# One row of padding and one weight slice: where a matmul's two operands lie in SBUF

## The chip, the cores and the metric

The kernel runs on one core of one Trainium2 chip. The metric is device time in microseconds (us) of one execution. The core's engines are named as the profile names them: PE (TensorE matmul), PEld (TensorE weight load), DVE (VectorE), ACT (ScalarE), POOL (GpSimd), SP (SyncE, which issues the DMAs here). SBUF is the on-chip memory that all of them read; every tile has a byte address there that is the same in each of the 128 partitions.

## The reference

A causal 7-tap filter over 4096 positions (its taps are a softmax, one set for each of 8 channel groups), and then two expert layers, one with h·cos(h), one with h·relu6(h+3)/6:

```python
x = attn_out.reshape(B * S, D)          # 4 * 4096 tokens, D = 192
h = x @ w_in                            # 192 -> 2048
g = h * np.cos(h)                       # second layer: h * clip(h + 3, 0, 6) / 6
return g @ w_out                        # 2048 -> 192
```

## The kernel before

Tokens are the moving (streamed) side: 32 blocks of N = 512 tokens, two layers, and 16 steps of 128 of the 2048 hidden channels for each block and layer, 1024 steps in all. Each float32 operand is held as a high and a low float32r part, so that one product takes several passes.

A step's **first product** (`mm1`, L636) makes `h`. It is done for two steps at once: 9 passes, each a pair of matmuls. One matmul of a pair works on rows 0 to 63 of the array, the other on rows 64 to 127 (`HALF`), and the two halves run beside each other. Its moving tiles are `own`, `swap` and `last` (4096 bytes a partition, four buffers each).

The **second product** (`mm2`) takes `gh` and `gl`, the high and the low part of the activation (2048 bytes a partition, four buffers each), and adds into four PSUM accumulators: a0 and a1 (`A`) for 128 output channels, b0 and b1 (`B`) for the other 64. A step has five passes, again pairs over the two halves of the rows: A with `gh` and the high weights, A with `gh` and the low weights, B with `gh` and 128 columns (64 high, 64 low: rows 0 to 63 and 64 to 127 of b hold the two, and are added at the end), A with `gl`, and B with `gl`. For this last one only the 64 high columns are needed. `half_wide` (L242) issues that matmul by hand with 64 weight columns, so that it writes rows 0 to 63 of b alone. [...]

So a step has 4.5 pairs of the first product and 5 of the second. Each matmul streams 512 columns and is preceded by a load of its own weights.

The order of all work is made ahead of time by a small planner (`Schedule.place`), which places operations by assumed costs and due times on each engine; it also chooses ACT or DVE for some casts (L257 on ACT, L259 on DVE). One matmul pair is assumed to take `MM = 0.2275` us there; this is a constant of the code and not a measurement.

**Addresses.** Tiles lie in SBUF in the order of their pools: weights (`wpool`), constants, `raw_p`, `x_p`, `g_p`. In the built program the weights of both layers start at 16512 and 65664 bytes, and all slices that a pass loads begin at a multiple of 256 bytes from there: their addresses leave the rest 128 modulo 256. The first tiles of `x_p` are one `xb` of `WIDE_B` floats and two `xa` of `WIDE_A` floats, of which 518 are used. All that comes after them in `x_p` and `g_p` (`own`, `swap`, `last`, `gh`, `gl`, and the activations' buffers) has sizes that are multiples of 256, so that `WIDE_A` and `WIDE_B` alone decide its rest. Before, it is 0 for each of them.

Ahead of the float32r stage, a few matmuls run in other forms. A warm-up (L767, bf16) reads weights and moving operand from the same place of one tile. Four filter blocks are done on TensorE in plain float32 over all 128 rows (`conv_pe`, L500): `xb` (rest 128) with diagonals (rest 192) twice, the second `xa` buffer (rest 224) with diagonals (rest 192), and the first `xa` buffer (rest 192) with diagonals (rest 192); tap i starts 4·i bytes further on.

Of the kernel before, what the change touches and what calls it, by code (L numbers as in the profile page):

```python
# [17 lines left out]
P = 128  # L18
D = 192
D2 = D - P  # L20
# [19 lines left out]
NW = 2 * D  # L40


WIDE_A, WIDE_B = 520, 528

UNBIAS_ON_ACT = 32
CAST_ON_ACT = 32
# [3 lines left out]
HALF = slice(0, D2), slice(D2, P)  # L50
# [153 lines left out]
def conv_cos_relu6_kernel(  # L204
# [13 lines left out]
    nc = tc.nc  # L218
# [9 lines left out]
    s = Schedule()  # L228
# [3 lines left out]
    def value(tag):  # L232
        return s.value(tag, BUFS[tag])

    def new(v, pool, dt, shape=(P, N)):
        v.data = pool.tile(list(shape), dt, tag=v.tag, name=v.tag, bufs=BUFS[v.tag])
        return v.data

    def half_wide(out, lhsT, rhs):

        pe = nc.tensor
        pe.add_instruction(  # L242
            mybir.InstMatmult(
                name=nc.get_next_instruction_name(),
                engine=mybir.EngineType.PE,
                start_tensor_calc=False,
                stop_tensor_calc=False,
                tile_size=(D2, P),
                tile_position=(rhs.base_partition(), 0),
                ins=[pe.lower_ap(rhs), pe.lower_ap(lhsT)],  # L250
                outs=[pe.lower_ap(out)],
            )
        )

    def cast(e, out, in_):
        if e == "act":
# [363 lines left out]
    START, MM = 12.0, 0.2275  # L620
# [70 lines left out]
    def mm2(t):  # L691
        l, b, j = steps[t]
        gh, gl = G.pop(t)
        if j == 0:
            ACC[l, b] = [value(n) for n in ("a0", "a1", "b0", "b1")]
        acc = ACC[l, b]
        A, B = acc[:2], acc[2:]
        first, last = j == 0, j == NJ - 1
        unit = WU[l, j - j % 2 + 1]
        w = W[l][:, j - j % 2 + 1, j % 2]  # L700

        def product(out, c, g, **flags):
            for i in range(2):
                w_i = w[HALF[i], c : c + P]
                nc.tensor.matmul(out[i].data, lhsT=w_i, rhs=g.data[HALF[i]], **flags)  # L705

        def high(e):
            if first:
                for v in acc:
                    new(v, ps_a, F32)  # L710
            product(A, 0, gh, start=first, stop=False)
            product(A, D + D2, gh, start=False, stop=False)
            if not last:
                product(B, P, gh, start=first, stop=False)

        def low(e):
            product(A, 0, gl, start=False, stop=last)
            for i in range(2):
                half_wide(B[i].data[:D2], w[HALF[i], P:D], gl.data[HALF[i]])
            if last:  # L720
                product(B, P, gh, start=False, stop=True)

        due = START + MM * (4.5 * min(NS, t + LAG + 2) + 5 * t)
        n = 2 if last else 3
        s.op({"pe": n * MM}, high, [gh, unit], acc, due=due)
        s.op({"pe": (5 - n) * MM}, low, [gl, gh, unit], acc, due=due + n * MM)

    def evac(l, b):
        a0, a1, b0, b1 = ACC.pop((l, b))
# [47 lines left out]
    for t in range(-26, NS + LAG):  # L777
        for u in range(t, t + 27):
            if 0 <= u < NS:
                l, b, j = steps[u]  # L780
                if (l, j) not in WU and (u <= t + 8 or l == 1):
                    weights(l, j)
                if l == 0 and j == 0 and b not in (x for _, x in X) and (b != 1 or u <= t + LOOK):
                    prepare(b)
        if 0 <= t < NS and t % 2 == 0:
            for i, h in enumerate(mm1(t)):
                middle(t + i, h)
        if t >= LAG:
            mm2(t - LAG)
            l, b, j = steps[t - LAG]  # L790
            if j == NJ - 1:
                evac(l, b)
# [56 lines left out]
```

## Time and profile before

| | us |
|---|---|
| median of 3 runs | 2318.5 (2316.7 to 2319.52) |
| the profiled execution: its time | 2316.11 |
| the profiled execution: span, first to last instruction | 2314.3 |
| PE busy in it | 2302.1 |
| PEld busy | 2066.3 |
| DVE, ACT, POOL busy | 1729.7, 1688.6, 1412.2 |

A matmul's record is longer than the distance to the next one, since matmuls are pipelined; what counts is the distance between the starts of two matmuls on the same half of the rows, called the spacing below. In the timeline the two halves alternate, so that it is the distance from one matmul record to the next but one. TensorE's clock was granted in full (2.4 GHz) in 0.999 of the time.

### The profile page before, as it was taken

The numbers are of one execution on the slowest core, as the hardware profiler recorded it, in microseconds if no ns is written. First come the engines' busy times: TensorE is split into PE (matmuls) and PEld (weight loads), VectorE is DVE, ScalarE is ACT, GpSimd is POOL, SyncE is SP. The second block draws the span as 40 slices with busy tenths as digits, with TensorE's granted clock in tenths as the row PEclk, the third lists the DMA queues.
The fourth block names the chain that finished last, engine by engine and source line by source line (L and its number), as shares of the span: only waits on it lengthen the run. The fifth ranks groups of instructions, "written<-read, shape, count | busy, mean of one in ns | idle before, by whom it ended". The sixth has DMA issues, their size and how long they took to land.

```text
span 2314.3 us, 49748 instructions
## 1 busy us (share of the span) xinstructions
PE 2302.1 (99%) x19564; PEld 2066.3 (89%) x19564; DVE 1729.7 (75%) x2318; ACT 1688.6 (73%) x2977; POOL 1412.2 (61%) x1049
## 2 busy tenths in 40 slices
PE   9999999999999999999999999999999999999998
PEld 4888899999999999999999999999999999999998
DVE  8898976877768777678777778777687776875553
ACT  5998677776777777777767777777777677777675
POOL 2666666666656666666666666666666665665555
PEclk9999999999999999999999999999999999999999
DMA  5322211111101111101111011111011110111000
GB/s 150 84 67 54 55 41 26 45 40 28 44 19 38 40 33 40 37 20 40 39 38 35 26 31 44 38 31 40 18 44 40 30 43 22 26 35 33 17 22 14
DMA packets 39130, 90.91 MB, mean 39 GB/s; under 512 B 6256, under 2 KB 12400, under 8 KB 38896
## 3 DMA queue, kind: packets, MB, share of 16 engines
q1 hardware_dynamic: 38896, 87.74, 14.7%
q8 instruction: 153, 2.51, 0.4%
q14 instruction: 81, 0.66, 0.1%
HBM read 25.32 MB, written 12.58 MB: 16 GB/s over the span
## 4 chain that ended last, share of the span: by engine, by line
PE 98%; DVE 1%; ACT 0%; DMA 0%; SPq 0%; issue 0%; DVEq 0%; ACTq 0%
PE h L636 46%; PE a L705 31%; PE b L705 10%; PE b L242 10%; PE h L500 1%; DMA raw<-w 0%; ACT r L663 0%; ACT da L311 0%; DVE w L262 0%; DVE last L262 0%; ACT w L257 0%; DVE r L666 0%; DVE swap L262 0%; DVE swap L259 0%; ACT k L655 0%
## 5 line engine op out<-in xcount | busy, mean ns | idle before, releaser
L262 POOL TENSOR_TENSOR gl<-r,gh 128x512 fp32r<-128x512 f32 x1024 | 1396.5, 1377 | 866.3 <-ACT gh L257 772.6
L705 PE MATMUL a<-gh,w 64*128 64x512 f32 x4096 | 904.3, 392 | 0.2 <-DVE w L262 0.2
L636 PE MATMUL h<-own,w 64*128 64x512 f32 x3072 | 877.6, 392 | 0.7 <-ACT own L257 0.7
L636 PE MATMUL h<-swap,w 64*128 64x512 f32 x3072 | 665.1, 392 | 3.4 <-DVE swap L259 1.9
L705 PE MATMUL b<-gh,w 64*128 64x512 f32 x2048 | 666.2, 393 | 0.0
L242 PE MATMUL b<-gl,w 64*64 64x512 f32 x2048 | 662.9, 390 | 0.0
L705 PE MATMUL a<-gl,w 64*128 64x512 f32 x2048 | 662.7, 389 | 0.0
L705 PEld LDWEIGHTS a<-gh,w 64*128 64x128 f32 x4096 | 594.7, 185 | 65.5 <-ACT da L311 0.8
L257 ACT ACTIVATE gh<-r 128x512 fp32r<-128x512 f32 x1024 | 619.5, 631 | 32.4 <-DVE r L666 25.5
L636 PEld LDWEIGHTS h<-own,w 64*128 64x128 f32 x3072 | 568.0, 185 | 33.7 <-ACT own L257 1.5
L675 ACT ACTIVATE r<-h,three 128x512 f32<-128x512 f32 x512 | 324.8, 684 | 361.2 <-PE h L636 327.9
L636 PE MATMUL h<-last,w 64*128 64x512 f32 x3072 | 570.7, 391 | 0.0
L660 DVE SCALAR_TENSOR_TENSOR r<-k,h 128x512 f32<-128x512 int32 x512 | 334.9, 682 | 253.5 <-ACT k L655 134.3
L636 PEld LDWEIGHTS h<-swap,w 64*128 64x128 f32 x3072 | 489.6, 185 | 31.6 <-DVE swap L259 2.2
L678 DVE SCALAR_TENSOR_TENSOR r<-r,h 128x512 f32<-128x512 f32 x512 | 327.7, 679 | 219.1 <-ACT r L675 218.8
L636 PEld LDWEIGHTS h<-last,w 64*128 64x128 f32 x3072 | 407.8, 185 | 29.8
L655 ACT ACTIVATE k<-h 128x512 int32<-128x512 f32 x512 | 280.6, 594 | 171.8 <-PE h L636 171.1
L705 PEld LDWEIGHTS a<-gl,w 64*128 64x128 f32 x2048 | 375.9, 185 | 20.3 <-issue 0.8
L705 PEld LDWEIGHTS b<-gh,w 64*128 64x128 f32 x2048 | 376.2, 185 | 18.9 <-DVE tb L739 0.6
L666 DVE TENSOR_TENSOR r<-r,h 128x512 f32<-128x512 f32 x512 | 339.1, 684 | 52.1 <-ACT r L663 51.8
L663 ACT ACTIVATE r<-r,half_pi 128x512 f32<-128x512 f32 x512 | 353.7, 721 | 24.5 <-DVE r L660 23.6
L242 PEld LDWEIGHTS b<-gl,w 64*64 64x64 f32 x2048 | 268.3, 132 | 19.8
(70 smaller groups left out, 1123.7 us busy)
## 6 DMA issues: line engine op xcount, KB each, us to landing
swap<-own SPq DMA_DIRECT2D x126, 256.0 KB, 3.7
last<-last SPq DMA_DIRECT2D x64, 256.0 KB, 3.1
xa<-xa SPq DMA_DIRECT2D x32, 259.0 KB, 2.7
outT<-ta SPq DMA_DIRECT2D x32, 256.0 KB, 2.0
raw<-w SPq DMA_DIRECT2D x16, 384.0 KB, 3.3
xb<-xb SPq DMA_DIRECT2D x16, 259.0 KB, 2.6
raw<-w SPq DMA_DIRECT2D x32, 128.0 KB, 2.7
outT<-u SPq DMA_DIRECT2D x32, 128.0 KB, 2.3
```

Of the source, the lines that this page charges most:

```text
L242: pe.add_instruction(mybir.InstMatmult(name=nc.get_next_instruction_name(), engine=mybir.EngineType.PE, start_tensor_calc=False, stop_tens ...
L257: nc.scalar.activation(out=out, in_=in_, func=AF.Copy)
L262: (nc.vector if e == "dve" else nc.gpsimd).tensor_tensor(out, a, b, op=ALU.subtract)
L500: nc.tensor.matmul(y.data, lhsT=tap(i), rhs=x.data[:, i : i + N], start=(i == 0), stop=(i == TAPS - 1),)
L636: nc.tensor.matmul(h.data, lhsT=w[HALF[i], pw, c * P : (c + 1) * P], rhs=moving[i][c][HALF[i], px], start=(n == 0), stop=(n == len(passes) ...
L655: nc.scalar.activation(out=new(k, g_p, I32), in_=h.data, func=AF.Copy, bias=0.25, scale=1.0 / TWO_PI)
L660: nc.vector.scalar_tensor_tensor(new(r, g_p, F32), k.data, TWO_PI, h.data, ALU.mult, ALU.subtract)
L663: nc.scalar.activation(out=r.data, in_=r.data, func=AF.Sin, bias=half_pi, scale=-1.0)
L666: nc.vector.tensor_tensor(r.data, r.data, h.data, op=ALU.mult)
L675: nc.scalar.activation(out=new(r, g_p, F32), in_=h.data, func=AF.Relu, bias=three, scale=1.0)
L678: nc.vector.scalar_tensor_tensor(r.data, r.data, 6.0, h.data, ALU.min, ALU.mult)
L705: nc.tensor.matmul(out[i].data, lhsT=w_i, rhs=g.data[HALF[i]], **flags)
```

## The change

The pad of `xb` grows from 528 to 560 floats, by 128 bytes. Every moving tile behind it moves by 128 bytes: `own`, `swap`, `last`, `gh` and `gl` now leave the rest 128 modulo 256, as the weights do. `half_wide` is gone: B with `gl` is an ordinary pass with 128 weight columns (64 high, 64 low), on all 128 rows of b, and the last step of a block keeps the order of the others.

```diff
-WIDE_A, WIDE_B = 520, 528
+WIDE_A, WIDE_B = 520, 560
...
-    def half_wide(out, lhsT, rhs):
-
-        pe = nc.tensor
-        pe.add_instruction(
-            mybir.InstMatmult(
...
             product(A, 0, gh, start=first, stop=False)
             product(A, D + D2, gh, start=False, stop=False)
-            if not last:
-                product(B, P, gh, start=first, stop=False)
+            product(B, P, gh, start=first, stop=False)
 
         def low(e):
             product(A, 0, gl, start=False, stop=last)
-            for i in range(2):
-                half_wide(B[i].data[:D2], w[HALF[i], P:D], gl.data[HALF[i]])
-            if last:
-                product(B, P, gh, start=False, stop=True)
+            product(B, P, gl, start=False, stop=last)
 
         due = START + MM * (4.5 * min(NS, t + LAG + 2) + 5 * t)
-        n = 2 if last else 3
-        s.op({"pe": n * MM}, high, [gh, unit], acc, due=due)
-        s.op({"pe": (5 - n) * MM}, low, [gl, gh, unit], acc, due=due + n * MM)
+        s.op({"pe": 3 * MM}, high, [gh, unit], acc, due=due)
+        s.op({"pe": 2 * MM}, low, [gl, unit], acc, due=due + 3 * MM)
```

On PE the program's order stays as it was nearly everywhere. Here is the last step of one block before (a is a0 and a1, b is b0 and b1; 64x512 or 128x512 is the size of the output):

```order
L705 MATMUL a_6183<-gh,w_78 128x512
L705 MATMUL a_6184<-gh,w_78 128x512
L705 MATMUL a_6183<-gh,w_78 128x512
L705 MATMUL a_6184<-gh,w_78 128x512
L705 MATMUL a_6183<-gl,w_78 128x512
L705 MATMUL a_6184<-gl,w_78 128x512
L242 MATMUL b_6185<-gl,w_78 64x512
L242 MATMUL b_6186<-gl,w_78 64x512
L705 MATMUL b_6185<-gh,w_78 128x512
L705 MATMUL b_6186<-gh,w_78 128x512
```

And the same step of the changed program:

```order
L689 MATMUL a_6189<-gh,w_78 128x512
L689 MATMUL a_6190<-gh,w_78 128x512
L689 MATMUL a_6189<-gh,w_78 128x512
L689 MATMUL a_6190<-gh,w_78 128x512
L689 MATMUL b_6191<-gh,w_78 128x512
L689 MATMUL b_6192<-gh,w_78 128x512
L689 MATMUL a_6189<-gl,w_78 128x512
L689 MATMUL a_6190<-gl,w_78 128x512
L689 MATMUL b_6191<-gl,w_78 128x512
L689 MATMUL b_6192<-gl,w_78 128x512
```

The pass of b with `gl` has 128 output rows in place of 64, and in the last step of a block it has changed places with the pass of b with `gh`; the count of matmuls is the same.

`low` no longer reads `gh`, which frees its buffer earlier in the planner's eyes, and so the planner fills the other engines in another order. The one shift of work between engines is the cast of `own` from the filtered block `ya`: 28 were on ACT and 1 on DVE, now 3 are on ACT and 26 on DVE. One of them on ACT before:

```order
L675 ACTIVATE r<-h,three 128x512 x2
L257 ACTIVATE gh<-r 128x512
L257 ACTIVATE own<-ya 128x512
L257 ACTIVATE gh<-r 128x512
L675 ACTIVATE r<-h,three 128x512 x2
```

and one on DVE after:

```order
L662 SCALAR_TENSOR_TENSOR r<-r,h 128x512 x8
L243 CAST own<-ya 128x512
L662 SCALAR_TENSOR_TENSOR r<-r,h 128x512 x2
L246 TENSOR_TENSOR own<-ya,own 128x512
L246 TENSOR_TENSOR last<-yb,last 64x512
```

What moved is the cast alone; the subtraction that makes the low part of `own` was on DVE before too.

## Rows read from the trace of the kernel before

**Rows 1.** The page: busy time of each engine, and the chain that ended last.

```profile
PE 2302.1 (99%) x19564; PEld 2066.3 (89%) x19564; DVE 1729.7 (75%) x2318; ACT 1688.6 (73%) x2977; POOL 1412.2 (61%) x1049
PE 98%; DVE 1%; ACT 0%; DMA 0%; SPq 0%; issue 0%; DVEq 0%; ACTq 0%
```

**Rows 2.** PE's waits in the whole span: us in total, times, longest.

```profile
PE h L636 <- DVE swap L259: 1.9, 1, 1.9
...
PE h L636 <- DVE swap L262: 0.8, 1, 0.8
...
PE h L636 <- ACT own L257: 0.7, 1, 0.7
```

**Rows 3.** Stretches: start:end, length, busy us (x instructions) by engine, clock, DMA share.

```profile
60.00:120.00 60.00, 59.20 (x505) 48.69 (x503) 53.27 (x86) 55.80 (x106) 38.41 (x31) 1.00 0.30 78
...
200.00:1200.00 1000.00, 1000.00 (x8612) 911.80 (x8610) 770.23 (x988) 724.06 (x1268) 625.62 (x456) 1.00 0.15 38
1200.00:2200.00 1000.00, 1000.00 (x8612) 913.53 (x8611) 730.76 (x946) 723.95 (x1268) 617.09 (x454) 1.00 0.13 32
```

**Rows 4.** The page's costliest groups of PE and PEld: busy, mean ns of one.

```profile
L705 PE MATMUL b<-gh,w 64*128 64x512 f32 x2048 | 666.2, 393 | 0.0
L242 PE MATMUL b<-gl,w 64*64 64x512 f32 x2048 | 662.9, 390 | 0.0
...
L705 PEld LDWEIGHTS b<-gh,w 64*128 64x128 f32 x2048 | 376.2, 185 | 18.9 <-DVE tb L739 0.6
...
L242 PEld LDWEIGHTS b<-gl,w 64*64 64x64 f32 x2048 | 268.3, 132 | 19.8
```

**Rows 5.** Timeline of PE in one step: start us, us of one, instruction.

```profile
1082.03 0.40 PE L705 MATMUL a<-gh,w 64*128 64x512 f32 x1
1082.23 0.39 PE L705 MATMUL a<-gl,w 64*128 64x512 f32 x1
1082.27 0.39 PE L705 MATMUL b<-gh,w 64*128 64x512 f32 x1
1082.46 0.39 PE L242 MATMUL b<-gl,w 64*64 64x512 f32 x1
...
1082.70 0.39 PE L705 MATMUL a<-gh,w 64*128 64x512 f32 x1
...
1082.92 0.42 PE L705 MATMUL a<-gh,w 64*128 64x512 f32 x2
1083.15 0.39 PE L705 MATMUL b<-gh,w 64*128 64x512 f32 x1
```

**Rows 6.** Timeline of PEld at the same place.

```profile
1082.01 0.18 PEld L705 LDWEIGHTS a<-gl,w 64*128 64x128 f32 x1
1082.03 0.19 PEld L705 LDWEIGHTS b<-gh,w 64*128 64x128 f32 x1
1082.24 0.13 PEld L242 LDWEIGHTS b<-gl,w 64*64 64x64 f32 x1
```

**Rows 7.** Timeline of PE in a first product with denser collisions.

```profile
1089.20 0.40 PE L636 MATMUL h<-own,w 64*128 64x512 f32 x1
...
1089.44 0.39 PE L636 MATMUL h<-own,w 64*128 64x512 f32 x1
...
1090.60 0.66 PE L636 MATMUL h<-last,w 64*128 64x512 f32 x4
```

**Rows 8.** Timeline of PE: three float32 filter blocks, 14 records each.

```profile
31.05 6.25 PE L500 MATMUL h<-xa,diag 128*128 128x512 f32 x14 [0.77 <-issue]
...
39.52 6.28 PE L500 MATMUL h<-xb,diag 128*128 128x512 f32 x14
...
46.63 6.28 PE L500 MATMUL h<-xa,diag 128*128 128x512 f32 x14
```

**Rows 9.** Casts of own, by tile: ns min/median/max, first and last start.

```profile
L257 ACT ACTIVATE own<-ya x28: 616/629/633, 96.5 to 2104.0; 128x512 fp32r<-128x512 f32 x28
...
L259 DVE CAST own<-ya x1: 1514/1514/1514, 356.1 to 356.1; 128x512 fp32r<-128x512 f32 x1
```

More of the change, by code (lines that the diff above doesn't have):

```diff
@@ L237, in new @@
         return v.data
-    def half_wide(out, lhsT, rhs):
-        pe = nc.tensor
-        pe.add_instruction(
-            mybir.InstMatmult(
[L244 to L253, printed above, removed]
     def cast(e, out, in_):
```

## The prediction

> **What bounds the kernel now.** I read the page first, from its top: PE is busy in 99% of the span and makes up 98% of the chain that ended last [rows 1]. Then PE's waits: beyond the start they come to a few single ones, the longest 1.9 us [rows 2]. In the two long stretches PE has no idle time at all, while DVE and ACT are busy 724 to 770 of 1000 us [rows 3]. So nothing that happens on DVE, ACT, POOL or the DMA queues can gain time, and PE's own pace is what is left to look at. This pace is the same in both stretches: 8612 matmuls, 4306 pairs, in 1000 us, which is a spacing of 0.2322 us. The kernel has 1024 steps of 9.5 pairs, 9728 pairs. One nanosecond of spacing is thus worth 9.7 us, 0.42% of the kernel.
>
> 512 columns at 2.4 GHz are 0.2133 us, so 0.019 us of each spacing are something else. The timeline shows two kinds of spacing. Around a pass with 64 weight columns it is quiet: from A with gl at 1082.23 over L242 at 1082.46 to B with gh at 1083.15 four spacings take 0.92 us, 0.230 each [rows 5]. Just before, the matmul at 1082.03 lasts 0.40 in place of 0.39 and is followed on its half at 1082.27, 0.24 later [rows 5]; the load that runs under it, from 1082.03, takes 0.19 and not 0.18 [rows 6]. Load and matmul on the same half are both longer at the same place: I read this as a collision of their reads, and call it so below, though no row says on what they wait. Elsewhere collisions are denser: from 1089.20 to 1090.60, six spacings take 1.40 us, 0.2333 each, and 0.23 and 0.24 follow each other [rows 7]. All of this is with rests 0 and 128.
>
> **The change part by part.** The sum is made against the profiled execution's 2316.1 us (span 2314.3 and 1.8 around it); the median of the runs is 2.4 us above.
>
> First, B with gl loads 128 columns. A load grows from 132 to 185 ns [rows 4], 2048 times, but both are shorter than the spacing of 230, and lie under the matmul before. So the load's length by itself costs nothing; the cover is the 45 ns that remain, and without it all of the 53 ns would show, 54 us over 1024 pairs. What may be lost is the quiet around the short load. All spacings together stand (0.2322 − 0.230) · 9728 = 21 us above quiet. The two spacings at each short load carry none of this, the other 7.5 of a step carry 21 us / 7680 = 2.8 ns each. If the two become like the others, that is 2048 · 2.8 ns = 6 us. The mean matmul points the same way, 390 ns for L242 and 393 for B with gh [rows 4]. A gain from loading more I exclude: nothing waits for the columns that are added. So 0 to +6 us, and I take 6 where collisions depend on the columns at all.
>
> Second, the rest. That moving operand and weights start at the same place modulo 256 bytes has no row of before in float32r. I bound it by the pace that rows show. Below: no collision at all, 0.230 everywhere, −21 us. Above: a collision in every spacing, 0.24 everywhere, (0.24 − 0.2322) · 9728 = +76 us; both bounds hold the first part in them. Between these, the nearest thing to a steady denser pattern is the stretch where every second spacing collides, 0.2333: (0.2333 − 0.2322) · 9728 = +11 us. I take this one, again with the first part in it, because it is the only denser pattern that the trace shows holding over several matmuls.
>
> Third, the planner's shifts. The 25 casts of `own` that go from ACT to DVE cost 0.63 us each on ACT and up to 1.51 on DVE [rows 9], at most 38 us on an engine with 230 us idle in each 1000 [rows 3]; without that cover each would come on top of a block's preparation. The main loop asks for a block's preparation up to 26 steps before its first matmul, some 50 us, and a wait would have to outlast that. The last step of a block swaps two passes: the accumulators a are complete one spacing later, b at the same time, and the span ends with b. I count 0. The order also changes in the first 120 us, where PE is not yet full (0.8 us idle from 60 to 120 [rows 3]); the waits there are single ones of 0.7 to 1.9 us [rows 2], so I allow 3 us to either side. Moved addresses of DMA targets touch transfers that keep the DMA engines busy 13 to 15% of the time in the long stretches [rows 3], and PE waits for none: 0.
>
> Sum: 2316.1 + 11 + 0 = 2327 in the profiled execution's terms, 2330 beside the median.
>
> **The rivals.** *The rest does nothing.* For it speaks a natural comparison in the trace: the filter blocks on TensorE read moving operand and weights with rests 224 and 192, 128 and 192, 192 and 192, and their 14 records take 6.25, 6.28 and 6.28 us [rows 8]. The block with equal rests is as fast as the one with unequal ones, to 0.03 us, or 2 ns a record. Against it: these are float32 matmuls over all rows, whose records follow each other at 6.28 / 14 = 0.45 us, twice the spacing, for the same 512 columns, so they read half as many bytes in a nanosecond; a stream with every second slot free may hide what a full one can't. It would give the first part alone, 0 to +6 us: 2318 to 2324, I say 2321. The Trainium skill says the same more strongly: "TensorE: Matmul & The Clock Gate", section "Step-by-step: what each phase is for", has two independent SBUF read ports, and says that loading the next weights takes no read bandwidth from the running matmul. By that rule both parts cost 0 and the time stays at 2318. The rows disagree with it in one point: a matmul and the load under it get longer together, and not beside a load of half the columns [rows 5, 6].
>
> *Equal rests are the better ones: faster.* If the two streams start at the same time from the same place modulo 256 and one runs ahead of the other, they may never meet within the 128 columns, where with a distance of 128 bytes they meet in the middle. For it speaks that there are collisions now, with unequal rests, and that half the columns meet none. It decides as soon as collisions become rarer than now by more than the 6 us of the first part: all quiet gives 0.230, 2316 − 21 = 2295, 2297 beside the median. The planner's constant of 0.2275 would give 2316 − 46 = 2270, but no stretch that I read goes on at that pace. Against it: the quiet spacing needs a short load in all rows that I have, and no short load is left.
>
> *Every spacing collides.* The streams would stay together over the whole load: +76 us, 2392, 2395 beside the median. Against it: two streams that stop each other once should be apart afterwards, and even the dense stretch has quiet spacings in between [rows 7].
>
> **How the numbers follow.** Denser collisions by a little, the forecast: 0.31. Denser up to every spacing: 0.17. The rest does nothing: 0.23. Rarer collisions: 0.29. A measurement of this kernel tells about 0.2%, 4.6 us, from no change. Slower takes the first two cases and a small part of the third, where the 6 us show in full: 0.50. Faster takes nearly all of the last, 0.28, and the same what is left, 0.22. The likeliest case gives 2330, its own range is 2322 to 2350. For 8 in 10 the range must reach into both outer cases: down to 2280, past the all-quiet 2297 toward the planner's pace, and up to 2385, short of the full +76.
>
> **What would show it.** In the profile after, the count of matmuls in 200 to 1200 us is the whole story: 8573 for the forecast (0.2333), 8612 if nothing changed, 8696 if all are quiet, 8333 if all collide. If the collision reading holds, matmuls of 0.40 over loads of 0.19 become more frequent in step with this, and appear around B with gl, whose mean goes from 390 toward 393 while its load goes to 185. If the third part is wrong, PE has new waits for `own` or `swap` after 120 us. The prediction is wrong if the pace moves without longer loads and matmuls, or below 0.230.

## The result and the profile after

| | before | after |
|---|---|---|
| median, us | 2317.60 (2316.41 to 2319.52, 4 runs) | 2278.04 (2276.68 to 2279.39, 4 runs) |
| the profiled execution: its time | 2316.11 | 2276.68 |
| its span | 2314.3 | 2275.0 |
| matmuls from 1200 to 2200 us | 8612 | 8828 |

The ratio is 0.9829, with a 95% interval of 0.9811 to 0.9846: 1.7% faster. The prediction said 2330 and slower. It had the sign wrong, and the time lies 2 us under its range.

The page, its engines, its chain and the costliest PE and PEld groups, as in [rows 1] and [rows 4]:

```profile
PE 2255.3 (99%) x19564; PEld 2018.1 (89%) x19564; DVE 1617.2 (71%) x2345; ACT 1745.5 (77%) x2953; POOL 1403.2 (62%) x1046
...
PE 93%; DVE 3%; ACT 2%; issue 1%; DMA 0%; SPq 0%; DVEq 0%; ACTq 0%
...
L689 PE MATMUL b<-gh,w 64*128 64x512 f32 x2048 | 645.6, 386 | 0.0
...
L689 PE MATMUL b<-gl,w 64*128 64x512 f32 x2048 | 644.8, 386 | 0.0
...
L689 PEld LDWEIGHTS b<-gl,w 64*128 64x128 f32 x2048 | 374.2, 184 | 21.5
```

There are as many matmuls as before, and PE is as full, but each matmul is shorter: 386 ns where [rows 4] had 393 and 390. The load of B with `gl` grew from 132 to 184 ns, as foreseen. The stretches (columns as in [rows 3]; the last is the GB/s that the DMA moved):

```profile
60.00:120.00 60.00, 55.37 (x459) 48.45 (x457) 49.89 (x81) 51.98 (x99) 34.63 (x27) 0.97 0.30 78
...
200.00:700.00 500.00, 497.17 (x4362) 441.65 (x4360) 373.99 (x515) 376.87 (x636) 320.81 (x234) 1.00 0.15 40
200.00:1200.00 1000.00, 997.17 (x8774) 899.00 (x8772) 732.67 (x1019) 760.07 (x1276) 635.97 (x466) 1.00 0.15 38
1200.00:2200.00 1000.00, 1000.00 (x8828) 914.71 (x8826) 686.43 (x985) 777.21 (x1298) 624.37 (x466) 1.00 0.13 33
```

Two things are to be read here. From 1200 to 2200 us PE never idles and does 8828 matmuls in 1000 us: the spacing is 2 · 1000 / 8828 = 0.2266 us, where it was 0.2322 [rows 3]. The granted clock is 1.00 in both, the upper level of 2.4 GHz, so it is not the clock. And early on something was lost: from 60 to 120 us PE does 459 matmuls where it did 505 [rows 3], and from 200 to 700 us it idles for 2.8 us, where it idled for none. PE's waits say for what:

```profile
PE h L620 <- DVE r L650: 2.5, 3, 1.4
PE h L620 <- DVE swap L243: 2.1, 1, 2.1
PE h L620 <- ACT w L241: 2.0, 1, 2.0
PE a L689 <- DVE ta L718: 1.4, 3, 0.7
PE h L746 <- DVE w L775: 1.3, 1, 1.3
PE a L689 <- DVE w L246: 1.2, 1, 1.2
```

The waits for `r`, for `w` at L241 and L246 (parts of the weights, cast and subtracted while the kernel already multiplies) and for `ta` are new or longer: before, PE waited 0.6 us for `r`, 0.2 for the same subtraction of `w`, and not at all for the other two.

The step that [rows 5] show, in the timeline of PE after:

```profile
1082.73 0.39 PE L689 MATMUL a<-gl,w 64*128 64x512 f32 x1
1082.76 0.39 PE L689 MATMUL b<-gh,w 64*128 64x512 f32 x1
1082.96 0.39 PE L689 MATMUL b<-gl,w 64*128 64x512 f32 x1
1082.98 0.39 PE L689 MATMUL a<-gl,w 64*128 64x512 f32 x1
1083.19 0.39 PE L689 MATMUL a<-gh,w 64*128 64x512 f32 x1
1083.21 0.39 PE L689 MATMUL b<-gl,w 64*128 64x512 f32 x1
1083.41 0.41 PE L689 MATMUL a<-gh,w 64*128 64x512 f32 x2
1083.64 0.39 PE L689 MATMUL b<-gh,w 64*128 64x512 f32 x1
...
1083.87 0.39 PE L620 MATMUL h<-own,w 64*128 64x512 f32 x1
```

From A with `gl` at 1082.73 on, one half goes 0.23, 0.23, 0.22, 0.23, 0.23: five spacings in 1.14 us, 0.228 each, and not one of 0.24. No matmul on this half stands out, B with `gl` included.

### The profile page after: what moved, and what is told of

Read it like the earlier page. It is cut to its first block, busy times and chain, and to the rows that moved or that the text cites. A ratio compares the mean times of both kernels' runs of the same rounds, so it can differ in the third digit from the quotient of the medians.

```text
span 2275.0 us, 50104 instructions
## 1 busy us (share of the span) xinstructions
PE 2255.3 (99%) x19564; PEld 2018.1 (89%) x19564; DVE 1617.2 (71%) x2345; ACT 1745.5 (77%) x2953; POOL 1403.2 (62%) x1046
## 4 chain that ended last, share of the span: by engine, by line
PE 93%; DVE 3%; ACT 2%; issue 1%; DMA 0%; SPq 0%; DVEq 0%; ACTq 0%
PE h L620 44%; PE a L689 29%; PE b L689 19%; PE h L484 1%; ACT k L639 0%; DMA raw<-w 0%; ACT gh L241 0%; DVE w L246 0%; DVE r L662 0%; DVE r L650 0%; ACT r L647 0%; DVE da L303 0%; DVE da L306 0%; DVE r L644 0%; DVE ya L421 0%
## 5 line engine op out<-in xcount | busy, mean ns | idle before, releaser
L246 POOL TENSOR_TENSOR gl<-r,gh 128x512 fp32r<-128x512 f32 x1024 | 1389.7, 1366 | 834.4 <-ACT gh L241 567.1
L689 PE MATMUL a<-gh,w 64*128 64x512 f32 x4096 | 879.1, 387 | 2.7 <-DVE ta L718 1.4
L620 PE MATMUL h<-own,w 64*128 64x512 f32 x3072 | 863.5, 387 | 4.3 <-ACT w L241 2.0
L241 ACT ACTIVATE gh<-r 128x512 fp32r<-128x512 f32 x1024 | 637.1, 631 | 170.4 <-PE b L689 61.3
L689 PE MATMUL b<-gh,w 64*128 64x512 f32 x2048 | 645.6, 386 | 0.0
L689 PE MATMUL a<-gl,w 64*128 64x512 f32 x2048 | 645.5, 387 | 0.0
L689 PE MATMUL b<-gl,w 64*128 64x512 f32 x2048 | 644.8, 386 | 0.0
L689 PEld LDWEIGHTS a<-gh,w 64*128 64x128 f32 x4096 | 585.1, 184 | 48.2 <-DVE ta L718 2.4
L620 PE MATMUL h<-last,w 64*128 64x512 f32 x3072 | 555.8, 387 | 0.0
L620 PEld LDWEIGHTS h<-last,w 64*128 64x128 f32 x3072 | 398.5, 185 | 32.8
L689 PEld LDWEIGHTS b<-gl,w 64*128 64x128 f32 x2048 | 374.2, 184 | 21.5
```

Source lines behind the costliest of these rows:

```text
L241: nc.scalar.activation(out=out, in_=in_, func=AF.Copy)
L246: (nc.vector if e == "dve" else nc.gpsimd).tensor_tensor(out, a, b, op=ALU.subtract)
L620: nc.tensor.matmul(h.data, lhsT=w[HALF[i], pw, c * P : (c + 1) * P], rhs=moving[i][c][HALF[i], px], start=(n == 0), stop=(n == len(passes) ...
```

## The experiments

Three theories were set against each other first. **A**: the distance between the two operands, modulo 256 bytes, decides. **B**: the moving operand's own rest decides. **C**: the gain comes from the even width, since no load of 64 columns is left between loads of 128. All times are medians, with the ratio to the kernel before on the same chip and its 95% interval. "Spacing" is 2 · 1000 us divided by the matmuls from 1200 to 2200 us of the profiled execution.

### Each part alone, and the weights moved instead

*rest_only* is the kernel before, `half_wide` and all, with the pad alone:

```diff
-WIDE_A, WIDE_B = 520, 528
+WIDE_A, WIDE_B = 520, 560
```

> The kernel before with the pad of 560 alone: moving operands and weights both leave the rest 128, B with gl still loads 64 columns. Theory A (the distance of the two operands modulo 256 sets the pace): spacing 0.2265 to 0.2275, 8790 to 8830 matmuls from 1200 to 2200 us, time 2270 to 2285. Theory C (the even width of all loads sets the pace): spacing 0.2322, 8612 matmuls, time 2317.

*width_only* is the changed kernel with the pad taken back, so that its operands are 128 bytes apart again:

```diff
-WIDE_A, WIDE_B = 520, 560
+WIDE_A, WIDE_B = 520, 528
```

> The changed kernel with the pad back at 528: moving operands leave 0, weights 128, every pass loads 128 columns. Theory A: the collisions stay and the quiet around the short load is lost, spacing 0.2322 to 0.2328, time 2316 to 2324. Theory C: spacing 0.2265, time 2278.

*weights_moved* is the changed kernel with three small constants put ahead of the weights. The weights move by 128 bytes; the moving tiles stay where the changed kernel has them, since the constants were taken from between the two. So moving operands and weights are 128 apart, with the rests exchanged: weights 0, moving 128.

```diff
-    half_pi = cpool.tile([P, 1], F32, tag="half_pi", name="half_pi")
-    three = cpool.tile([P, 1], F32, tag="three", name="three")
+    half_pi = wpool.tile([P, 1], F32, tag="half_pi", name="half_pi")
+    three = wpool.tile([P, 1], F32, tag="three", name="three")
+    sw_t = wpool.tile([P, 2, TAPS], F32, tag="sw", name="sw")
```

> The changed kernel with 128 bytes of small constants put ahead of the weights, and the pad of 560 kept: moving operands leave 128 as in the changed kernel, weights leave 0. Theory A: spacing 0.2322 to 0.2328, time 2316 to 2324, and matmuls of 0.40 over loads of 0.19 are back. Theory B: spacing 0.2265, time 2278.

*both_at_0* has the same move and the pad of 528: weights 0, moving 0.

> The changed kernel with 128 bytes of small constants put ahead of the weights and the pad at 528: moving operands and weights both leave 0. Theory A: spacing 0.2265, time 2278. Theory B (the moving operand's own rest sets the pace, 128 is good and 0 is bad): spacing 0.2322 to 0.2328, time 2316 to 2324.

| | weights, moving | us | ratio | spacing, us |
|---|---|---|---|---|
| rest_only | 128, 128 | 2283.57 | 0.9858 (0.9841 to 0.9874) | 0.2287 |
| width_only | 128, 0 | 2329.57 | 1.0056 (1.0038 to 1.0074) | 0.2332 |
| weights_moved | 0, 128 | 2326.70 | 1.0044 (1.0029 to 1.0059) | 0.2323 |
| both_at_0 | 0, 0 | 2278.85 | 0.9837 (0.9822 to 0.9851) | 0.2266 |

A holds; B falls, and C falls as the cause by itself. The kernel is fast wherever the rests are equal, at 128 or at 0, and not where they differ, whichever operand has which. The rest alone, with the loads of 64 columns still there, is worth 32.9 us (2316.4 to 2283.6). *width_only* and *weights_moved* also have the new order of the work, which costs time by itself (see below), so that width alone is to be read from their spacings: 0.2332 and 0.2323, no gain over 0.2322. Some figures lie outside what A had let expect: the spacing of *rest_only* is above 0.2275, the spacing of *width_only* above 0.2328, and the times of *width_only* and *weights_moved* above 2324.

*weights_moved* and *both_at_0* differ in the pad alone. PE's stretches (length, PE busy, clock, DMA share, GB/s) of the first:

```profile
1200.00:2200.00 1000.00, 1000.00 (x8610) 1.00 0.13 34
```

and of the second:

```profile
1200.00:2200.00 1000.00, 1000.00 (x8826) 1.00 0.13 33
```

In *weights_moved* the pattern of [rows 5, 6] is back. In PE's timeline the matmuls at 1081.76 and 1081.77, one on each half, take 0.40. On the first of these halves 0.23 (from 1081.53) and 0.24 (to 1082.00) follow each other; the row at 1082.00 holds two records, so its 0.40 is not the length of one:

```profile
1081.53 0.39 PE L620 MATMUL h<-swap,w 64*128 64x512 f32 x1
...
1081.76 0.40 PE L620 MATMUL h<-swap,w 64*128 64x512 f32 x1
1081.77 0.40 PE L620 MATMUL h<-own,w 64*128 64x512 f32 x1
1082.00 0.40 PE L620 MATMUL h<-swap,w 64*128 64x512 f32 x2
```

The two loads beside them, one row of PEld's timeline, take 0.19 together (188 ns each in the trace), the next one 0.18:

```profile
1081.77 0.19 PEld L620 LDWEIGHTS h<-swap,w 64*128 64x128 f32 x2
1082.01 0.18 PEld L620 LDWEIGHTS h<-own,w 64*128 64x128 f32 x1
```

*rest_only* also shows what the 64 columns do once the rests are equal. Its groups from 200 to 2200 us:

```profile
L636 PE MATMUL h<-own,w 64*128 64x512 f32 x2760 | 772.9, 386 | 0.0
...
L242 PE MATMUL b<-gl,w 64*64 64x512 f32 x1841 | 569.4, 394 | 0.0
L705 PE MATMUL b<-gh,w 64*128 64x512 f32 x1841 | 565.2, 390 | 0.0
```

and PE's timeline in a second product:

```profile
1082.81 0.39 PE L705 MATMUL a<-gl,w 64*128 64x512 f32 x1
...
1083.04 0.39 PE L242 MATMUL b<-gl,w 64*64 64x512 f32 x1
...
1083.28 0.39 PE L705 MATMUL a<-gh,w 64*128 64x512 f32 x1
...
1083.50 0.40 PE L705 MATMUL a<-gh,w 64*128 64x512 f32 x2
1083.74 0.39 PE L705 MATMUL b<-gh,w 64*128 64x512 f32 x1
```

The first product is at 386 ns as in the changed kernel; the matmuls around the short load are not, and 0.24 appears behind it, twice. Before, this very place was the quiet one. So the short load is not quiet by itself: it breaks the even pace of equal rests, and was no worse than the rest only while every spacing was uneven.

*width_only* is spread more than the others: its four executions took 2333.03, 2326.11, 2324.80 and 2333.55, and the spacing in the table is that of the first. *weights_moved*, with the same program order, keeps the 0.2322 of before and is still 10.3 us slower than it; this comes back below.

The long matmuls over long loads don't go with the pace, though. From 1200 to 2200 us the trace of the kernel before has 964 matmuls of 398 ns or more and 964 loads of 128 columns of 187 ns or more, that of *weights_moved* 1230 of each, that of the changed kernel none. But *width_only*, slower than the first two, has none of either: its matmuls take 388 or 395 ns, its loads 184.

### How equal must the rests be?

*dist_m64*, *dist_m32* and *dist_p32* are the changed kernel with other pads, so that the moving operands lie 64 or 32 bytes under or 32 over the weights' rest. The version of A in which equality alone is free is called A1.

```diff
-WIDE_A, WIDE_B = 520, 560
+WIDE_A, WIDE_B = 520, 544      # dist_m32: 552, dist_p32: 568
```

> The changed kernel with a pad of 544: moving operands leave 64, weights 128, 64 bytes apart. If only equal rests are free of collisions (A1): spacing 0.230 to 0.2335, time 2300 to 2330. If the pace worsens with the distance (A2): half way, spacing about 0.230, time about 2303. If any distance but 128 is good (A3): spacing 0.2265, time 2278.

> The changed kernel with a pad of 552: moving operands leave 96, weights 128, 32 bytes apart. A1: spacing 0.230 to 0.2335, time 2300 to 2330. A2: spacing about 0.228, time about 2291. A3: spacing 0.2265, time 2278.

> The changed kernel with a pad of 568: moving operands leave 160, weights 128, 32 bytes apart on the other side. A1: spacing 0.230 to 0.2335, time 2300 to 2330. A2: spacing about 0.228, time about 2291; A3: 2278. If the two sides differ, it is the order in which the streams pass each other that counts, and not the distance alone.

| distance, bytes | us | ratio | matmuls, 1200 to 2200 us |
|---|---|---|---|
| −64 | 2332.10 | 1.0067 (1.0048 to 1.0087) | 8574 |
| −32 | 2335.77 | 1.0079 (1.0059 to 1.0099) | 8574 |
| +32 | 2336.50 | 1.0080 (1.0060 to 1.0100) | 8574 |

All three have one pace, 0.2333, within what A1 let expect; the times lie 2 to 6.5 us above its 2330. There is no slope: a small distance is as bad as a large one. Here too no matmul of 398 ns and no load of 187 ns is in the traces from 1200 to 2200 us.

Then smaller ones, with both layers' weights in one tile that begins some floats further on. *dist_16* has weights 144 and moving 128:

```diff
-WIDE_A, WIDE_B = 520, 560
+WIDE_A, WIDE_B = 520, 552
...
-    W = [wpool.tile([P, NJ, 2, NW], F32R, tag=f"w{l}", name=f"w{l}") for l in range(2)]
+    both = wpool.tile([P, 2 * NJ * 2 * NW + 8], F32R, tag="w0", name="w0")[:, 4 : 4 + 4 * NJ * NW]
+    both = both.rearrange("p (l j k c) -> p l j k c", l=2, j=NJ, k=2)
+    W = [both[:, l] for l in range(2)]
```

> The changed kernel with the weights of both layers in one tile, 16 bytes further on (rest 144), moving operands at 128: 16 bytes apart. If the rests must be equal to the byte: like 32 bytes apart, spacing 0.2325 to 0.2335, time 2320 to 2340. If a small distance, within some line that is read at once, is as good as none: spacing 0.2265, time 2275 to 2282.

*dist_4* begins one float further on in place of four: weights 132, moving 128.

> The same with 4 bytes, one element (rest 132 against 128). Equal to the byte: spacing 0.2325 to 0.2335, time 2320 to 2340. Same line is enough: spacing 0.2265, time 2275 to 2282. If 16 is slow and 4 is fast, the line is shorter than 16 bytes or lies across the 16.

*dist_4* took 2326.70, ratio 1.0036 (1.0023 to 1.0049), at a spacing of 0.2322: one element of distance is enough to lose all of it. *dist_16* took 2335.79 and 2335.15 in two executions and 2279.32 in a third, so its median says little and no ratio is given. Its profile, of the execution of 2335.79, has the slow pace:

```profile
1200.00:1700.00 500.00, 500.00 (x4288) 1.00 0.14 35
```

That one distance gives either pace is not explained; only the distances from 32 bytes up, 4 and 0 have one answer. The single tile for both layers was not run at distance 0; that it allows the fast pace, the third execution of *dist_16* shows.

### Does it act where the operand lies, or on the whole kernel?

*first_apart* has the pad of 528, and widens one buffer between the tiles of the first and the second product, so that `own`, `swap` and `last` are 128 apart from the weights, and `gh` and `gl` 0 apart:

```diff
-WIDE_A, WIDE_B = 520, 560
+WIDE_A, WIDE_B = 520, 528
...
-        s.op({"act": 0.52}, lambda e: cast(e, new(u, x_p, F32)[:D2], tb.data[D2:P]), [tb], [u])
+        def other_half(e):
+            u.data = new(u, x_p, F32, (P, N + 32))[:, :N]
+            cast(e, u.data[:D2], tb.data[D2:P])
+
+        s.op({"act": 0.52}, other_half, [tb], [u])
```

> The changed kernel with the pad at 528 and 128 bytes behind the last tile of x_p, so that own, swap and last leave 0 (128 apart from the weights) and gh and gl leave 128 (equal). If a collision is between one moving operand and the weights loaded under it: the passes of the first product go at about 0.2332 and those of the second at 0.2265, time 2278 + 4.5 * 1024 * 6.7 ns = 2309. If one pace holds for the whole stream, whichever operand sets it: 2278 or 2325.

It took 2312.79, ratio 0.9979 (0.9969 to 0.9989). PE's timeline, the beginnings of a first and a second product and of the next first one:

```profile
1502.88 0.39 PE L620 MATMUL h<-own,w 64*128 64x512 f32 x1
...
1507.07 0.85 PE L689 MATMUL a<-gh,w 64*128 64x512 f32 x4
...
1511.17 0.39 PE L620 MATMUL h<-own,w 64*128 64x512 f32 x1
```

Each of the two stretches holds 36 matmuls, 18 spacings. The first product takes 4.19 us, 0.2328 each; the second, with equal rests, 4.10 us, 0.2278 each. The cost is paid mostly product by product, where the two operands of that product differ. Not wholly: the second product stays 1.2 ns above 0.2266, and the time 4 us above the 2309 expected.

### What the new order of the work costs

*old_plan* is the changed kernel in which `low` names `gh` again among what it reads. It still doesn't read it; the planner then makes the order of before: row for row on DVE, POOL and SP, with 28 casts of `own` on ACT again, and on PE but for the last step of a block.

```diff
-        s.op({"pe": 2 * MM}, low, [gl, unit], acc, due=due + 3 * MM)
+        s.op({"pe": 2 * MM}, low, [gl, gh, unit], acc, due=due + 3 * MM)
```

> The changed kernel, but the planner is told again that the low passes read gh, so that it makes the order of before (28 casts of own on ACT) on all engines. If the new order costs PE the waits seen in its first 200 us (PE busy 55.4 of the 60 us from 60 to 120, and 997.2 of 1000 from 200 to 1200, against 59.2 and 1000 before): PE busy about 59 of 60 again, time 2268 to 2274. If those waits come from the quicker pace and not from the order: 2276 to 2280.

It took 2263.96 (2263.59 to 2265.12), ratio 0.9771 (0.9757 to 0.9784): 14.1 us less than the changed kernel, 4 us under the range expected, and the fastest version here. PE's stretches (length, PE busy, clock, DMA share, GB/s):

```profile
60.00:120.00 60.00, 58.94 (x509) 1.00 0.32 82
...
200.00:700.00 500.00, 500.00 (x4414) 1.00 0.16 41
700.00:1200.00 500.00, 500.00 (x4415) 1.00 0.14 36
```

The pace is that of the changed kernel, 4415 matmuls in 500 us. The difference is in the first 700 us: 509 matmuls against 459 from 60 to 120 us, where the changed kernel's granted clock is also 0.97 against 1.00, and 4414 against 4362 from 200 to 700 us. The first is 25 pairs · 0.2266 = 5.7 us, the second 26 pairs, 5.9 us. Together they are about the 11.6 us by which the two profiled executions differ (2276.68 and 2265.12). Of the waits of the changed kernel, the one for `w` at L241 is gone, those at L246 fall from 1.5 to 0.3 us, those for `r` from 2.5 to 0.6 and those for `ta` from 1.4 to 0.3; the longest one for `swap` is much the same in all three kernels (1.9 before, 2.1, 1.8):

```profile
PE h L620 <- DVE swap L243: 1.8, 1, 1.8
PE h L746 <- DVE w L775: 1.3, 1, 1.3
PE h L620 <- ACT own L241: 0.7, 1, 0.7
PE h L620 <- DVE r L650: 0.6, 1, 0.6
```

In the changed kernel's timeline of PE the wait for `w` at L241 begins like this:

```profile
73.91 0.39 PE L689 MATMUL b<-gl,w 64*128 64x512 f32 x2
76.30 0.50 PE L620 MATMUL h<-own,w 64*128 64x512 f32 x1 [2.00 <-ACT w L241]
...
76.64 0.39 PE L620 MATMUL h<-own,w 64*128 64x512 f32 x1
```

The wait itself is 2.00 us, and the first matmul behind it takes 0.50, with 0.34 to the next on its half. After two more waits, for `r`, of 0.79 and 1.42 us at 89.5 and 91.4, the granted clock falls: it is 0.83 from 90 to 100 us, where a part runs at the lower level of 1.2 GHz, and *old_plan*'s is 1.00 all the way from 60 to 120. So the cost is more than PE's idle time shows.

*old_plan_2265* has the planner reckon with the measured pace as well:

```diff
-    START, MM = 12.0, 0.2275
+    START, MM = 12.0, 0.2265
```

> The same, and the planner's cost of a pair set to the pace measured, 0.2265 for 0.2275. If the plan's pace matters by as little as 0.4%: within 2 us of the run without it. If due times that fit better take away waits: up to 3 us faster.

It took 2267.12, ratio 0.9782 (0.9769 to 0.9795), 3.2 us more than *old_plan*, neither of the two outcomes expected. That the planner's pace had come to be off is not what costs the 14 us.

## Why the prediction was wrong

**The second term, the rest, failed, and with it the sign.** The prediction bounded it by −21 us, "no collision at all, 0.230 everywhere", and took +11 as "the nearest thing to a steady denser pattern". Measured beside loads of 64 columns it is −32.9 us (*rest_only*), beside loads of 128 columns −47.9 (*weights_moved* to *both_at_0*) to −51.5 (*width_only* to the changed kernel). Two things were wrong. The floor was no floor: 0.230 around the short load was the lowest pace that the prediction had read among unequal rests, and equal rests give 0.2266. And the pattern of dense collisions was chosen because it was the only one to be seen, though it too was a row of unequal rests; no row could say on which side equal ones lie. The prediction's own sign of being wrong, a pace below 0.230, is what came.

**The first term, 128 columns, had a gain excluded that was there.** "Nothing waits for the columns that are added" is true, and still the change from 64 to 128 columns at equal rests goes from *rest_only*'s 2283.6 to *old_plan*'s 2264.0, −19.6 us, with the planner's order of before in both (the two also differ in the order of PE's last step of a block, and ran on two chips, where the kernel before took 2316.4 and 2317.3). By the spacings it is (0.2287 − 0.2266) · 9728 = 20 us. At unequal rests the columns give between no change of spacing (*weights_moved*, 0.2323) and +0.001 us (*width_only*, 0.2332, some +10 us), which is about what the term said. The two edits depend on each other, and were costed as if they did not.

**The third term, the planner's shifts, was sized at 0, ±3, and measured +14.1.** It argued with the idle time of DVE and ACT in each 1000 us and with 50 us of lead. The loss is at single places early on, where PE waits for weights, `r` and `ta`, and not for `own` or `swap`, which the prediction had named; the mean over 1000 us says nothing on them. *weights_moved* shows the same with the pace of before: 10.3 us more than the kernel before, at an equal spacing. Which of the moved operations makes `w` late was not tried.

The three, −32.9 − 19.6 + 14.1, make −38.4 us. That this is 2278.0 − 2316.4 is no check of them: they are steps on one path, from the kernel before (as it ran beside *rest_only*) over *rest_only* and *old_plan* to the changed kernel, and on another path the single sizes differ, as the −47.9 and −51.5 show.

**The rivals.** "Equal rests are the better ones" was right in kind, with 0.29, and its 2297 was too small a gain for the reason above. Its other figure, 2270 at the planner's pace of 0.2275, came near the measured pace, but it is a constant of the code, so that this was luck and no reading; and the argument against it, that "the quiet spacing needs a short load in all rows", is what *rest_only* refutes. "The rest does nothing" is refuted by *rest_only*. The Trainium skill's rule from "TensorE: Matmul & The Clock Gate", section "Step-by-step: what each phase is for", that loading the next weights takes no read bandwidth from the running matmul, does not agree with these runs: *weights_moved* and *both_at_0* have the same loads and the same order on PE, and differ by 47.9 us in where the moving operand lies. The comparison that had spoken for it, the plain float32 filter blocks, could hardly have shown a difference. Tap i of a block starts 4·i bytes further on, so that in the block that was read as one of equal rests only one of the seven taps has them, and *dist_4* shows that one element of distance loses the fast pace in the float32r stream. The three blocks of [rows 8] take 6.25, 6.28 and 6.28 us after as before, where the pad has taken the equal rests from that one tap too; this says little for the same reason.

**What stays open.** That two reads collide was argued from a matmul and a load that grow together; the experiments only show that the distance of their addresses decides, and the slowest pace, 0.2333, comes without such matmuls and loads. Whether the load meets the matmul on its own half or on the other one was not tried. Nor is it known why unequal rests give now 0.2322, now 0.2333. The 0.2266 is still 13 ns above the 0.2133 of 512 columns at 2.4 GHz.

## What to carry to other kernels

Where float32r matmuls on halves of the rows follow each other without a gap, each with its own load of weights, look at the addresses of both operands modulo 256 bytes, for each product, and pad one tile until the rests are equal to the element; look again after every change of the allocation. A pace that the trace shows is a bound only for the conditions under which it was seen, so a stretch that looks undisturbed is no floor for a change of the condition itself. After an edit that also changes what a planner is told, run it once with the planner's order of before: here that was worth another 14 us.

## What the runs showed of the hardware

The start spacing of paired float32r matmuls on 64 rows, 512 columns each, with loads of 128 columns and the clock granted in full, is 0.2266 us where the moving operand and the weights leave the same rest modulo 256 bytes (0 and 0, 128 and 128), and 0.2322 to 0.2333 at distances of 4, 32, 64 and 128 bytes; at 16 bytes single executions took one pace or the other (2279 and 2335 us). A load of 64 columns among those of 128 raises the mean spacing at equal rests to 0.2287. Whether plain float32 matmuls on 128 rows show anything of this is open: in the filter blocks at most one tap of seven had equal rests.
